# Exclusive decay sums on VectorE, and a state update split between VectorE and GpSimd

## The chip and the metric

The kernel runs on one core of a Trainium2 chip. A core has five engines that matter here: PE (TensorE, matrix multiplication), DVE (VectorE), ACT (ScalarE), POOL (GpSimd) and SP, which only issues transfers. Each works through its own queue of instructions in order, and waits on semaphores for the others. PSUM, where PE writes its results, has 8 banks of 512 float32 per partition; GpSimd has no operand in PSUM anywhere in this kernel.

The metric is the device time of one execution in microseconds (us); less is better. Before the change the median of 7 runs is 213.39 us (212.85 to 214.91).

## What is computed

Two layers, one after the other. The first is a recurrence over 768 steps, for 4 batches and 8 heads of width 40, with a 40 x 40 state per head:

```
for t in range(S):
    y[:, :, t] = einsum('bhd,bhde->bhe', rt, state)
    Sa = einsum('bhde,bhe->bhd', state, at)
    state = state * wt[:, :, None, :] - einsum('bhd,bhe->bhde', Sa, bt) \
            + einsum('bhd,bhe->bhde', vt, kt)
```

The second takes y as x of shape (4, 768, 320) and mixes it over tokens and channels:

```
theta = x @ w_theta
y = einsum('ts,bsd->btd', w_tok_r, x * cos(theta)) + einsum('ts,bsd->btd', w_tok_i, x * sin(theta))
u = x + y
out = u + maximum(u @ w_ch, 0)
```

## The kernel before

The 768 steps of each batch are cut into 6 chunks of 128, so there are N = 24 chunks; chunk i is the chunk `i % 6` of batch `i // 6`. Inside a chunk the recurrence is written as matrix products. Time steps lie on the 128 partitions, and heads and channels (DM = 320 columns) along the free axis. The loops are these:

- `loads(i)` issues the six input loads of a chunk (w, k, b, a, v, and r for two chunks at a time) on SP's queue.
- `prep(i)` makes what a chunk needs before the recurrence. ACT takes the logarithm of w into `lw` (L659). `cs` on PE sums it over time with triangular matrices of ones: L666 with `ntri_inc` gives minus the inclusive sums, L668 with `tri_exc` (the strictly triangular `mask_p`) the exclusive sums, L670 and L674 the total of the chunk, with off-diagonal blocks set to a large negative number. These fill a tile of two PSUM banks, placed so that they are 648 neighbouring columns, and one ACT exp (L678) turns them all into `ex`: the inverse inclusive decay `invW`, the exclusive decay `Wi`, and the decay of the whole chunk `wm`. POOL (DVE for the first two chunks) multiplies k and b by `invW` (kb, L686) and a by `Wi` (ah, L690). PE transposes the results (L616) and ACT copies them out of PSUM (L619).
- `attention_scores(i)` makes 128 x 128 score matrices per head on PE, four kinds in all (`scores`, L740, with 64-row operands, so that PE changes its tiling mode before and after), and DVE multiplies each by a triangular mask (L745). Each uses a two-bank tile.
- `recurrence(i)` makes x0 (from the old state `gt_old` and from v), nx, nu, and, unless the chunk is the last of its batch, the new state: PE adds the old state into the accumulation by a product with the identity (L804, not for the first chunk of a batch), then adds the products of kb with v and nu (L809), and DVE multiplies the sum by `wm` into `gt_new` (egt, L817). The state's transposes (gd) and the next chunk's x0 wait for it.
- `readout(i)` makes the output y on PE (L863 to L872), which DVE multiplies by `Wi` (ex, L879); `theta(i)` makes the angles; `sines` takes cosine and sine on ACT, with another activation table, half a batch at a time, and POOL makes the products z (L924).
- `mix_row` makes one 128-token row of the token mixing of a batch (L942: 12 matmuls of 320 columns) and of the channel mixing (L888), and stores it. The mixer's weights come by POOL's queue (`mixer_weights`, `wtok_block`) and are transposed on PE.

None of this runs in the order of the code. Every operation is added to a `Plan` with an engine, an estimated cost, what it reads and writes, and a priority made of due times (`TIMES`, `OFF`) and a table of single corrections (`ADJ`). `order` builds one static list from these, in which the instructions of every engine then stand. It gives out the PSUM banks too: four banks serve as two double tiles (`ps_d`), the other four as single ones (`ps_s`). In the first microseconds PE gets matmuls on a tile of ones, whose results are not used, ahead of certain operations (`WARM`, L598).

Of the kernel before, what the change touches and what calls it, by code (L numbers as in the profile page):

```python
# [25 lines left out]
WARM = {("tv", 0): (512, 512, 512, 512, 512, 512, 256), ("cs", 0): (256, 128),  # L26
        ("ta", 0): (512, 512, 512, 256, 128), ("spsi", 0): (512, 256, 128), ("cs", 1): (128, 128),
        ("x0", 0): (256, 128)}
# [199 lines left out]
def mm(n):  # L228
    return max(n / 2.4 + 2.5, 25.0)


def tail(n):
# [4 lines left out]
    ah=-35.84, ch=48.62, cs=-41.07, ea=8.9, egd=-133.96, egt=-68.6, ekb=29.91, enu=-49.74,  # L237
    enut=-31.32, er=-1.07, eth=-44.84, eut=-81.74, ev=34.77, ewt=-21.29, ex=-16.18, exp=-69.77,
    ext=-70.75, gd=-0.66, gt=24.57, kb=0.69, la=-21.49, lb=-20.79, lk=-21.05, ln=-58.38,
    loadr=-19.57, lv=-18.31, lw=-23.25, mlu=77.8, mlv=20.57, mphi=99.76, mpsi=106.6, nu=-4.03,  # L240
    nut=17.1, nx=-102.76, oo=44.39, r=13.19, row=39.85, sin=86.4, slu=-21.92, slv=29.13,
    sphi=-34.9, spsi=-25.62, st=34.46, ta=-13.27, th=35.87, tkb=6.76, tr=-5.45, tv=13.16,
    uadd=-11.95, ut=33.59, v=-54.81, wdma=85.37, wt=32.27, x0=-18.91, xt=5.58, y=-25.18,
    z=50.36)
WAIT, TSWITCH, PSWITCH = 398.44, 188399.0, -3357.0
TIMES = dict(
    tile=[
        -65.18, -52.14, -27.19, -15.19, -0.09, 16.27, 18.34, 39.82, 40.75, 43.08, 49.45, 52.18,
        68.94, 83.98, 96.98, 120.81, 109.42, 127.8, 136.07, 145.79, 151.2, 162.31, 163.45,
        185.34],  # L250
    row=[
        43.16, 28.13, 30.47, 7.23, 53.69, 54.58, 93.52, 93.6, 115.41, 121.11, 101.85, 144.65,
        150.48, 155.04, 152.8, 117.63, 86.15, 91.69, 209.97, 231.59, 245.27, 311.99, 320.81,
        183.2],
    rel=[
        -80.1, 35.36, 62.13, 56.14, -154.77, 90.95, 23.01, 50.8])
ADJ = {
    0: 0.01, 1: -0.88, 2: -0.27, 3: -0.13, 4: -9.48, 5: 1.93, 6: 0.01, 7: -6.64, 8: -6.95,
    9: 2.16, 10: -0.5, 11: 4.59, 12: 0.14, 13: 0.14, 14: -2.05, 15: 1.86, 16: 1.1, 17: 0.1,
    18: 0.09, 19: -1.57, 20: -11.2, 21: 2.84, 22: -9.69, 23: 4.35, 24: 11.96, 25: -7.67,  # L260
    26: -8.16, 27: -0.64, 28: 7.64, 29: -2.2, 30: 9.61, 31: -5.25, 32: -7.79, 33: 1.01,
    34: 0.1, 35: 13.97, 36: 2.59, 37: 8.9, 38: -2.75, 39: -7.81, 40: -5.57, 41: -1.21,
    42: -0.06, 43: 0.97, 44: 0.99, 45: 4.55, 46: -1.08, 47: 23.46, 48: 0.44, 49: 12.19,
    50: -0.53, 51: 9.26, 52: -2.79, 53: 0.97, 54: -23.89, 55: 7.88, 56: 2.16, 57: 5.54,
    58: 1.4, 59: 0.22, 60: 1.28, 61: -5.88, 62: -2, 63: -5.35, 64: 13.13, 65: -1, 66: 0.41,
    67: -1.73, 68: 4.62, 69: -0.84, 70: -7.71, 71: -0.16, 72: 4.87, 73: -0.18, 74: 3.79,
    75: 4.43, 76: 0.74, 77: 0.06, 78: 6.38, 79: -6, 80: -2.91, 81: 0.43, 82: 3.27, 83: 3.51,
    84: -0.44, 85: -2.07, 86: -2.74, 87: -2.44, 88: 2.94, 89: -22.98, 90: 3.09, 91: 9.21,
    92: -2.91, 93: 18.56, 94: 11.17, 95: -1.31, 96: -4.33, 97: -0.08, 98: 3.45, 99: 0.12,
    100: -1.86, 101: -0.16, 102: -12.32, 103: 7.19, 104: -6.11, 105: 0.71, 106: -14.73,  # L270
    107: -16.11, 108: -1.26, 109: -2.12, 110: -11.67, 111: 2.03, 112: -15.5, 113: -2.82,
    114: -4.71, 115: -1.47, 116: -2.37, 117: -4.76, 118: 13.45, 119: 10.68, 120: -10.01,
    121: 0.33, 122: 3.27, 123: -1.43, 124: 0.58, 125: -0.44, 126: -0.16, 127: -0.19,
    128: -0.03, 129: 9.47, 130: 3.96, 131: -3.42, 132: 7.74, 133: 20.39, 134: -13.3, 135: -2.8,
    136: -0.48, 137: -9.35, 138: 10.49, 139: -7.17, 140: 0.63, 141: 3.26, 142: -15.88,
    143: -0.69, 144: 2.2, 145: 3.25, 146: -0.52, 147: -2.19, 148: 0.82, 149: -2.89, 150: -2.96,
    151: -1.81, 152: -2.3, 153: 7.23, 154: 2.47, 155: 0.06, 156: 7.19, 157: 4.58, 158: 4.32,
    159: 9.96, 160: -1.9, 161: -3.25, 162: -5.02, 163: -0.81, 164: 6.53, 165: -0.05,
    166: -0.93, 167: -6.53, 168: 5.68, 169: -19.35, 170: -5.08, 171: -3.95, 172: 0.37,
    173: 0.24, 174: -0.2, 175: 0.06, 176: 2.16, 177: 2.88, 178: 0.56, 179: 8.74, 180: 1.39,  # L280
    181: -3.81, 182: 0.11, 183: 0.36, 184: -4.66, 185: 9.47, 186: 2.08, 187: -11.66,
    188: -0.63, 189: 0.85, 190: -0.92, 191: 10.42, 192: -9.45, 193: 13.4, 194: 6.74,
    195: -6.65, 196: -5.88, 197: -0.72, 198: 2.12, 199: -14.95, 200: 3.42, 201: -0.02,
    202: 1.83, 203: -7.04, 204: 6.08, 205: 5.21, 206: -3.71, 207: -2.32, 208: 13.41,
    209: -9.87, 210: 3.64, 211: 10.51, 212: 5.22, 213: 5.88, 214: -4.25, 215: 19.91,
    216: -0.01, 217: 5.8, 218: -8.62, 219: -2.51, 220: 10.26, 221: -2.18, 222: -2.47,
    223: 0.31, 224: -7.04, 225: -7.58, 226: -0.03, 227: -0.65, 228: -0.12, 229: 0.29,
    230: -0.2, 231: -2.85, 232: -6.4, 233: 2.09, 234: 2.03, 235: 0.33, 236: -1.18, 237: 1.09,
    238: 2.44, 239: -1.72, 240: 4.57, 241: 9.13, 242: -7.24, 243: 5.72, 244: -13.82, 245: 4.4,
    246: 0.42, 247: -0.19, 248: -6.12, 249: 1.82, 250: 1.83, 251: 1.17, 252: -1.48,  # L290
    253: -20.54, 254: 7.17, 255: -4.93, 256: 11.2, 257: -1.77, 258: 0.66, 259: -5.47, 260: 1.6,
    261: -0.4, 262: -3.63, 263: -6.81, 264: -3.82, 265: 0.49, 266: 6.09, 267: -2.63, 268: 1.75,
    269: -21.15, 270: 2.29, 271: 5.91, 272: 2.21, 273: 2.4, 274: -0.3, 275: -0.28, 276: -1.01,
    277: -0.05, 278: 0.09, 279: -0.7, 281: 11.01, 282: 0.43, 283: -2.64, 284: -0.86,
    285: -0.06, 286: 1.73, 287: 9.89, 288: 3.49, 289: -0.39, 290: -18.78, 291: 3.31, 292: 4.17,
    293: 4.49, 294: -5.08, 295: 6.91, 296: 3.6, 297: -3.29, 298: 0.56, 299: 10.13, 300: 1.9,
    301: -2.58, 302: -4.97, 303: 1.42, 304: 2.99, 305: -5.36, 306: -7.27, 307: -0.95,
    308: 1.82, 309: -1.14, 310: -0.67, 311: 14.01, 312: -5.86, 313: -0.01, 314: 1.39,
    315: -14.81, 316: -3.16, 317: -9.85, 318: 22.47, 319: -0.79, 320: 0.71, 321: 6.65,
    322: -0.13, 323: -5.53, 324: 7.33, 325: -2.66, 326: 5.7, 327: 1.43, 328: -0.19, 329: -0.19,  # L300
    330: -0.05, 331: -0.22, 332: -0.54, 333: 7.79, 334: -6.85, 335: 33.42, 336: -8.67,
    337: -0.3, 338: -1.27, 339: -5.14, 340: 6.36, 341: 0.65, 342: -20.61, 343: -0.78,
    344: -5.3, 345: -1.21, 346: 9.39, 347: 2.01, 348: -1.89, 349: 10.51, 350: 13.01, 351: -0.2,
    352: -3.48, 353: 4.69, 354: 4.84, 355: -1.57, 356: 1.1, 357: 0.4, 358: -0.66, 359: 0.59,
    360: 7.35, 361: 4.46, 362: -2.04, 363: 4.08, 364: 9.63, 365: 5.54, 366: 7.55, 367: -1.41,
    368: 2.55, 369: 8.31, 370: 0.16, 371: 5.97, 372: -0.62, 373: -2.28, 374: 5.86, 375: -13.84,
    376: -0.34, 377: 1.21, 378: -4.65, 379: 0.4, 380: -1.31, 381: 1.92, 382: -0.18, 383: -0.48,
    384: 0.4, 385: 0.18, 386: -2.48, 387: -14.19, 388: -4.1, 389: 0.04, 390: 0.77, 391: 1.61,
    392: -2.08, 393: -6.37, 394: 0.62, 395: 16.84, 396: 1.46, 397: -1.21, 398: -0.93,
    399: -15.78, 400: -1.89, 401: 7.32, 402: 0.61, 403: -3.23, 404: -4.29, 405: 27.28,  # L310
    406: 1.3, 407: 11.93, 408: -0.22, 409: -2.74, 410: -0.38, 411: 7.07, 412: 0.78, 413: -6.17,
    414: -4.48, 415: -8.05, 416: -4.72, 417: 0.39, 418: -2.8, 419: 10.74, 420: 12.65,
    421: 11.4, 422: 1.61, 423: -5.66, 424: -5.98, 425: 0.9, 426: -1.8, 427: -4.21, 428: -7,
    429: -2.07, 430: 3.36, 431: 4.59, 432: -1.73, 433: -1.81, 434: 6.99, 435: 5.71, 436: 10.27,
    437: 5.14, 438: -0.99, 439: 7.81, 440: 0.8, 441: 1.27, 442: 1.65, 443: 7.35, 444: -5.64,
    445: -1.46, 446: -7.08, 447: 0.09, 448: 13.81, 449: -2.33, 450: 2.41, 451: -7.56,
    452: -0.44, 453: 5.63, 454: 12.16, 455: -15.32, 456: -2.4, 457: 4.6, 458: 1.31,
    459: -12.31, 460: -0.7, 461: -1.77, 462: -0.69, 463: 0.39, 464: 0.12, 465: -1.48,
# [139 lines left out]
def kernel(  # L458
# [144 lines left out]
    def add(eng, kind, i, fn, cost, reads=(), writes=(), at="tile", **kw):  # L603
        if (kind, i) in WARM:
            fn = warmed(kind, i, fn, kw["new"][0])
# [465 lines left out]
```

## Time and profile before

The profiled execution took 213.0 us, with a span of 211.2 us on the core. The busy times:

| Engine | Busy us | Share of the span | Instructions |
|---|---|---|---|
| PE | 198.5 | 94% | 3365 |
| DVE | 166.2 | 79% | 253 |
| ACT | 152.1 | 72% | 342 |
| POOL | 117.6 | 56% | 173 |

The loads and stores on SP's queue moved 27.54 MB and took 66.6% of the time of the 16 DMA engines. Most of their packets are under 512 bytes. These are the lines that the change touches:

| Line | Engine, what | Count | Mean ns |
|---|---|---|---|
| L668 | PE, exclusive sums | 24 | 299 |
| L804 | PE, old state times identity | 16 | 300 |
| L678 | ACT, exp of 648 columns | 24 | 713 |
| L817 | DVE, state times decay | 20 | 486 |
| L598 | PE, matmuls on ones | 21 | 218 to 544 |

A line of the profile's groups gives source line, engine, operation, the tile written and the tiles read with their shapes, the count, the busy time and the mean of one, and then how long the engine sat idle ahead of it and for whom. Matmuls run in a pipeline: their durations overlap, and the starts of neighbours tell more of their price than the durations.

### The profile page before, as it was taken

What the parts mean: (1) busy time and instruction counts of PE and PEld (TensorE: products, weight loads), DVE (VectorE), ACT (ScalarE), POOL (GpSimd) and SP (SyncE); (2) the same over time, 40 slices, a digit from 0 to 9 for tenths busy, and PEclk for the clock granted to TensorE, in tenths of its full rate; (3) what the DMA queues carried; (4) which work ended last, traced back from release to release, by engine and by line L of the source; (5) the groups of instructions that cost most, each with busy time, mean ns of one, the idle gap of its engine ahead of it and who ended that gap; (6) DMA issues with size and microseconds to landing.
All of it is one profiled execution on the core that took longest, in us unless ns stands there. A gap on an engine that the chain in (4) does not pass through costs nothing.

```text
span 211.2 us, 8102 instructions
## 1 busy us (share of the span) xinstructions
PE 198.5 (94%) x3365; PEld 155.6 (74%) x3365; DVE 166.2 (79%) x253; ACT 152.1 (72%) x342; POOL 117.6 (56%) x173
## 2 busy tenths in 40 slices
PE   7668999989999999999999999999999999999993
PEld 3456787767777787788887877788778787877761
DVE  7578778896979799789897677878789898946343
ACT  4475877999799769967948789777898757573011
POOL 3205375798888674895971859763658440751000
PEclk9999999999999999999999999999999999999998
DMA  7999999899999999995979889888997101002122
GB/s 121 196 176 180 153 215 176 143 174 170 198 173 201 192 191 184 175 169 77 260 154 185 168 144 217 141 185 162 215 180 139 34 3 33 3 3 95 70 89 93
DMA packets 134181, 30.82 MB, mean 146 GB/s; under 512 B 125824, under 2 KB 134144, under 8 KB 134144
## 3 DMA queue, kind: packets, MB, share of 16 engines
q1 hardware_dynamic: 131712, 27.54, 66.6%
q0 software_dynamic: 2432, 2.77, 9.1%
q8 instruction: 26, 0.43, 0.8%
q14 instruction: 11, 0.09, 0.1%
HBM read 29.13 MB, written 3.93 MB: 157 GB/s over the span
## 4 chain that ended last, share of the span: by engine, by line
PE 76%; DVE 5%; SPq 5%; ACT 5%; POOL 3%; DMA 2%; issue 2%; ACTq 0%; POOLq 0%; DVEq 0%
PE ps_s L942 19%; PE ps_s L616 13%; PE ps_d L740 10%; PE ps_s L888 9%; SPq L635 4%; PE ps_s L843 4%; DMA raw_w<-in_w_dram 2%; PE ps_s L723 2%; PE ps_s L809 2%; DVE phi L745 2%; PE ps_s L990 2%; PE ps_s L791 2%; PE ps_s L872 2%; ACT ex L678 2%; PE ps_s L870 2%
## 5 line engine op out<-in xcount | busy, mean ns | idle before, releaser
L686 POOL TENSOR_TENSOR kb<-raw_kb,ex 128x320 bf16<-128x320 f32 x44 | 37.2, 862 | 19.1 <-ACT ex L678 17.7
L942 PE MATMUL ps_s<-zr,wtok_r 128*128 128x320 bf16 x144 | 41.0, 300 | 0.0
L942 PE MATMUL ps_s<-zi,wtok_i 128*128 128x320 bf16 x144 | 40.9, 299 | 0.0
L690 POOL TENSOR_TENSOR ah<-raw_a,ex 128x320 bf16<-128x320 f32 x22 | 19.0, 863 | 30.2 <-ACT ex L678 12.7
L745 DVE TENSOR_TENSOR lamu<-ps_d,mask_p 128x1024 bf16<-128x1024 f32 x24 | 29.3, 1219 | 7.0 <-PE ps_d L740 6.6
L745 DVE TENSOR_TENSOR phi<-ps_d,mask_n 128x1024 bf16<-128x1024 f32 x24 | 29.3, 1219 | 4.5 <-PE ps_d L740 4.2
L745 DVE TENSOR_TENSOR lamv<-ps_d,mask_p 128x1024 bf16<-128x1024 f32 x24 | 29.2, 1218 | 3.9 <-PE ps_d L740 3.7
L745 DVE TENSOR_TENSOR psi<-ps_d,mask_p 128x1024 bf16<-128x1024 f32 x24 | 29.2, 1216 | 1.5 <-PE ps_d L740 1.5
L924 POOL TENSOR_TENSOR zi<-cs,x 128x320 bf16<-128x320 f32 x23 | 17.8, 792 | 10.1 <-ACT cs L912 9.9
L924 POOL TENSOR_TENSOR zr<-cs,x 128x320 bf16<-128x320 f32 x23 | 17.8, 792 | 5.8 <-ACT cs L912 5.8
L678 ACT ACTIVATE ex<-ps_d 128x648 f32<-128x648 f32 x24 | 17.1, 713 | 4.8 <-PE ps_d L674 3.6
L619 ACT COPY uT<-ps_s 128x192 f32<-128x192 f32 x24 | 7.5, 319 | 15.5 <-PE ps_s L843 14.2
L879 DVE TENSOR_TENSOR x<-ps_s,ex 128x320 bf16<-128x320 f32 x24 | 11.7, 486 | 7.6 <-PE ps_s L872 3.5
L740 PE MATMUL ps_d<-aT,kbT 64*128 64x128 bf16 x384 | 16.6, 218 | 0.9 <-ACT kbT L619 0.7
L942 PEld LDWEIGHTS <-wtok_r 128*128 128x128 bf16 x144 | 14.0, 97 | 4.5
L942 PEld LDWEIGHTS <-wtok_i 128*128 128x128 bf16 x144 | 14.1, 98 | 3.5
L619 ACT COPY kbT<-ps_s 128x512 f32<-128x512 f32 x24 | 14.2, 590 | 3.3 <-PE ps_s L616 3.2
L952 DVE TENSOR_TENSOR u<-ps_s,x 128x320 bf16<-128x320 f32 x24 | 11.7, 489 | 6.0 <-PE ps_s L942 5.3
L961 DVE SCALAR_TENSOR_TENSOR oo<-ps_s,u 128x320 f32<-128x320 f32 x24 | 11.6, 488 | 5.2 <-PE ps_s L888 4.5
L870 PE MATMUL ps_s<-kb,lamv 128*128 128x40 bf16 x192 | 15.4, 181 | 0.0
L872 PE MATMUL ps_s<-kb,lamu 128*128 128x40 bf16 x192 | 15.0, 180 | 0.1
L616 PE MATMUL ps_s<-ident,kb 128*128 128x128 bf16 x192 | 14.7, 220 | 0.1
(117 smaller groups left out, 562.1 us busy)
## 6 DMA issues: line engine op xcount, KB each, us to landing
raw_v<-in_v_dram SPq DMA_DIRECT2D x24, 160.0 KB, 3.7
raw_w<-in_w_dram SPq DMA_DIRECT2D x24, 160.0 KB, 4.6
raw_kb<-in_k_dram SPq DMA_DIRECT2D x24, 160.0 KB, 3.8
raw_a<-in_a_dram SPq DMA_DIRECT2D x24, 160.0 KB, 4.6
raw_kb<-in_b_dram SPq DMA_DIRECT2D x24, 160.0 KB, 4.4
raw_r<-in_r_dram SPq DMA_DIRECT2D x24, 160.0 KB, 3.4
out_dram<-oo SPq DMA_DIRECT2D x24, 160.0 KB, 2.3
wrow_i<-in_moe_w_tok_i_dram POOLq DMA_DIRECT2D x6, 192.0 KB, 4.9
```

Of the source, the lines that this page charges most:

```text
L616: nc.tensor.transpose(out=dst[:, c:c + 128], in_=pair(src, g), identity=ident)
L619: nc.scalar.copy(out=out.bitcast(FP32), in_=in_)
L678: add("ACT", "exp", i, lambda: nc.scalar.activation(out=ex, in_=ps(pk).rearrange("p a b -> p (a b)")[:, 512 - DM:512 + DM + 8], func=AF.Ex ...
L686: lambda j=j: (nc.vector if fast else nc.gpsimd).tensor_tensor(out=paired(kb[:, j])[:, :, :, 0:D], in0=natural(raw_kb[s4][:, j]), in1=invW ...
L690: lambda: (nc.vector if fast else nc.gpsimd).tensor_tensor(out=paired(ah)[:, :, :, 0:D], in0=natural(raw_a[i % 6]), in1=Wi, op=ALU.mult),
L740: nc.tensor.matmul(t[:, q, g, :], lhsT=lhs[rows(q), g * 128:(g + 1) * 128], rhs=rhs[rows(q), g * 128:(g + 1) * 128], start=True, stop=True)
L745: add("DVE", kindm, i, lambda: nc.vector.tensor_tensor(out=dst.rearrange("p a b c -> p (a b) c"), in0=ps(p).rearrange("p a (g c) -> p (a g ...
L870: nc.tensor.matmul(o, lhsT=lamv[:, p, g, :], rhs=kb[:, 0, h, 0:D], start=first, stop=False, skip_group_check=True)
L872: nc.tensor.matmul(o, lhsT=lamu[:, p, g, :], rhs=kb[:, 1, h, 0:D], start=False, stop=True, skip_group_check=True)
L888: nc.tensor.matmul(dst, lhsT=lhs[:, kt, :], rhs=rhs[:, kt, :], start=kt == 0, stop=kt == 2)
L924: nc.vector if fast else nc.gpsimd).tensor_tensor(
L942: nc.tensor.matmul(ps(pk)[:, 0:DM], lhsT=wtok[nm][:, s, j * 128:(j + 1) * 128], rhs=zs[c][:, s], start=n == 0 and c == 0, stop=n == NT - 1 ...
```

## The change

It has four parts.

1. The exclusive sums are no longer made by PE. L668 goes. The inclusive sums and the totals (328 columns) now fit one bank, and `cs` takes a single bank instead of a double tile. Since the exclusive sum is the inclusive one less the step's own logarithm, DVE adds `lw` to minus the inclusive sum (`wi`, into the new tile `sx`), and a second exp on ACT with scale -1 makes `Wi` into the new tile `we` (`ew`). The exp of the inclusive sums and the total keeps its place, and `wi` is ordered after it. ah (L690) and the output multiplication (L879) read `we` in place of `ex`.
2. From chunk 4 on, for chunks that are neither first nor last of a batch (13 of them), PE does not add the old state by the identity (L804). DVE adds it when it takes the sum out of PSUM, into a new float32 tile `sum`, and POOL multiplies by `wm` into the new state (`wgt`). The other chunks keep the old way.
3. The matmuls on ones at the start are placed by the plan's own times, in steps of 128 columns wherever the plan leaves PE idle before 14 us, instead of a written list.
4. All due times, priorities and corrections of the plan are replaced (`OFF`, `TIMES`, `ADJ`, and the three weights), so that the order of instructions changes on every engine.

```diff
-WARM = {("tv", 0): (512, 512, 512, 512, 512, 512, 256), ("cs", 0): (256, 128),
...
+FROM_POOL = 4
+WARM_FROM, WARM_TO, WARM_STEP = 1450.0, 14000.0, 107.0
...
-            nc.tensor.matmul(t[:, 0, 512 - DM:512], lhsT=ntri_inc, rhs=lw[:, :, 0:D],
+            nc.tensor.matmul(t[:, 0:DM], lhsT=ntri_inc, rhs=lw[:, :, 0:D],
                              start=True, stop=True)
-            nc.tensor.matmul(t[:, 1, 0:DM], lhsT=tri_exc, rhs=lw[:, :, 0:D],
-                             start=True, stop=True)
...
-        add("ACT", "exp", i, lambda: nc.scalar.activation(
-            out=ex, in_=ps(pk).rearrange("p a b -> p (a b)")[:, 512 - DM:512 + DM + 8],
-            func=AF.Exp), 710, [pk], [kex], table="lnexp")
+        got = add("ACT", "exp", i, lambda: nc.scalar.activation(
+            out=ex, in_=ps(pk)[:, 0:DM + 8], func=AF.Exp), 440, [pk], [kex], table="lnexp")
+        kw, we, sx = ("we", i % NEX), we_t[i % NEX], sx_t[i % 2]
+        add("DVE", "wi", i, lambda: nc.vector.tensor_tensor(
+            out=sx.rearrange("p (h d) -> p h d", h=H),
+            in0=ps(pk)[:, 0:DM].rearrange("p (h d) -> p h d", h=H), in1=lw[:, :, 0:D], op=ALU.add),
+            490, [pk, ("lw", s2)], [("sx", i % 2)], after=[got])
+        add("ACT", "ew", i, lambda: nc.scalar.activation(out=we, in_=sx, func=AF.Exp, scale=-1.0),
+            455, [("sx", i % 2)], [kw], table="lnexp")
...
+            by_pool = not first and i >= FROM_POOL
+            join = not first and not by_pool
...
-                if not first:
+                if join:
                     nc.tensor.matmul(t[:, 0:DM], lhsT=ident,
...
+            if by_pool:
+                add("DVE", "egt", i, lambda: nc.vector.tensor_tensor(
+                    out=sum_t, in0=grown(),
+                    in1=gt_old.rearrange("p g c d -> p (g c) d")[:, :, 0:D], op=ALU.add), 490,
+                    [gk, ("gt", (i + 1) % 2)], [("sum", 0)])
+                add("POOL", "wgt", i, lambda: nc.gpsimd.tensor_tensor(
+                    out=new_state, in0=sum_t, in1=wm.to_broadcast([128, 8, D]), op=ALU.mult), 830,
+                    [("sum", 0), ("ex", i % NEX)], [("gt", s2)])
...
+    idle = WARM_FROM
     for o in order:
+        if o.eng == "PE" and o.start < WARM_TO:
+            if o.new is not None:
+                t = ps(o.new[0])
+                t = t[:, 0] if len(t.shape) == 3 else t
+                for _ in range(int((o.start - idle) / WARM_STEP)):
+                    nc.tensor.matmul(t[:, 0:128], lhsT=busy[:, 0:128], rhs=busy[:, 0:128],
+                                     start=True, stop=True, skip_group_check=True)
+            idle = o.start + 1.5 * o.cost + 50
```

## The prediction

> **What bounds the kernel now.** I read the page's busy times and slices first, then the same engines in five stretches cut at the landmarks of the trace, then who waited for whom in each stretch.
>
> ```profile
> PE 198.5 (94%) x3365; PEld 155.6 (74%) x3365; DVE 166.2 (79%) x253; ACT 152.1 (72%) x342; POOL 117.6 (56%) x173
> ...
> PE   7668999989999999999999999999999999999993
> ...
> DVE  7578778896979799789897677878789898946343
> ACT  4475877999799769967948789777898757573011
> ...
> DMA  7999999899999999995979889888997101002122
> ```
>
> PE is at 94%, but the average hides two regimes, which the stretches show (columns: length, then busy time and instructions of PE, weight loads, DVE, ACT, POOL, then granted clock, DMA share, GB/s):
>
> ```profile
> 0.00:24.00 24.00, 18.17 (x265) 12.55 (x265) 17.12 (x61) 14.45 (x32) 7.00 (x19) 1.00 0.95 171
> 24.00:56.00 32.00, 29.86 (x597) 24.21 (x594) 26.81 (x31) 27.54 (x66) 24.28 (x33) 1.00 0.95 173
> 56.00:71.00 15.00, 13.74 (x285) 11.60 (x283) 13.92 (x18) 13.40 (x30) 11.20 (x18) 1.00 1.08 192
> 71.00:163.00 92.00, 91.93 (x1620) 74.22 (x1617) 76.16 (x98) 74.56 (x167) 62.49 (x88) 1.00 0.93 175
> 163.00:206.00 43.00, 43.00 (x601) 32.12 (x599) 30.39 (x47) 21.54 (x51) 12.60 (x16) 1.00 0.12 41
> ```
>
> From 71.0, when the first token-mixing row (L942) issues, to 206, PE is busy 134.93 of 135 us, and the waits of PE list none in that time. There a PE instruction removed is time removed, as long as the others still feed it. Before 71 PE has gaps (its listed waits sum to 7.8 us, behind ACT, DVE and the start), DVE is at 84 to 93% and the DMA engines at 95% and more: several things share the limit there. The last input load is issued at 159.0, so that 43 us of PE work follow the loads: the end is PE's.
>
> A matmul's row overstates its price, since matmuls overlap. The decay sums of one chunk in the timeline (start, duration):
>
> ```profile
> 144.52 0.30 PE L666 MATMUL ps_d<-lw,ntri_inc 128*128 128x320 bf16 x1
> 144.66 0.30 PE L668 MATMUL ps_d<-lw,mask_p 128*128 128x320 bf16 x1
> 144.79 0.17 PE L670 MATMUL ps_d<-off_diag,ident 128*128 128x8 bf16 x1
> ```
>
> The next one starts 0.133 us after L668, not 0.30. So L668 costs 0.133 us of PE, and by the same width so does L804.
>
> **What goes from PE.** 24 matmuls of L668, and 13 of the 16 of L804 (chunks 4 and up that are neither first nor last of a batch): 37 x 0.133 = 4.9 us (by their means of 300 ns it would be 11.1, which the timeline refutes). I split them at the first row, since only behind it is PE the limit.
>
> Behind it stand 13 of L668 and 10 of L804: 23 x 0.133 = 3.06 us less. But the instructions are reordered as a whole. In the built order of the changed kernel a little more of the other work stands behind the first row: eight more L779 matmuls, eight L791, four L773 and four transposes, six more transposes of the mixer's weights, eight scores fewer: at their issue intervals (columns / 2.4 GHz at the granted clock of 1.00, at least 0.025; 0.034 a score) +0.8 us. And PE goes between the 64-row scores (L740) and full-height matmuls 77 times there, instead of 70. One such switch costs about 0.1 us (the last L872 starts at 146.08, the first score at 146.19, where 0.03 would do): +0.7. Sum behind the first row: -3.06 + 0.8 + 0.7 = **-1.6 us**.
>
> Ahead of it 11 of L668 and 3 of L804 go: 14 x 0.133 = 1.9 us. Worth between all of it (PE is busy for 92% of 56 to 71) and nothing (DMA and DVE set the pace). I take half, **-0.9**. The warm-up matmuls (21 before, 3.0 us at issue intervals; 68 of 128 columns, 3.6 us after) lie in PE's idle start, cover: the first chunk's loads and vector work. I cost them at 0; if that cover fails, +0.6.
>
> **What comes on DVE.** 24 additions from PSUM to SBUF at 128x320. The nearest row is L817, same shape and sources, 486 ns. Back to back it is less:
>
> ```profile
> 26.00 1.23 DVE L745 TENSOR_TENSOR lamu<-ps_d,mask_p 128x1024 bf16<-128x1024 f32 x1
> 27.14 1.22 DVE L745 TENSOR_TENSOR lamv<-ps_d,mask_p 128x1024 bf16<-128x1024 f32 x1
> 28.27 0.48 DVE L879 TENSOR_TENSOR x<-ps_s,ex 128x320 bf16<-128x320 f32 x1
> ```
>
> Masks follow each other by 1.13, and where the timeline has a 320-wide one followed at once it is 0.40. So +9.6 us of DVE in all, 0.4 a chunk. Behind the first row 12 to 14 of them, 5.4 us, fall on a DVE with 28.5 us idle: covered, 0. Ahead of it: up to the output multiplication of chunk 5 (sixth L879, 55.5), from which the first batch's sines and so the first row follow, the new order has 10 additions and one more mask but one state update fewer, 4.7 us; DVE is idle for 5.2 of the 32 us from 24 to 56 and for more before. Between 0 and +4.7. I take 0, because the idle time is just enough and the row start has slack of its own (theta of chunk 5 is evacuated at 58.9, and its sines start at 63.1, behind other ACT work and a table load).
>
> **ACT.** One exp of 648 columns (713 ns) becomes one of 328 and one of 320. Nearest rows: 128x320 ACTIVATE and COPY, 427 to 478. Sum 0.9, i.e. +0.18 by durations and +0.1 after the overlap of 0.1 that each ACT instruction has with the next; x24 = 2 to 4.5 us on an engine with 17 us idle behind the first row: 0. The table loads stay at 14. ah now waits for exp, addition and second exp: about 1 us more than before. Behind it in POOL's queue stand kb and v of later chunks, and PE's transposes of ah. But the new order has 3 to 10 us of PE work between a chunk's decay sums and its ah transposes (before: 1.2 to 5.6), so that stays covered.
>
> **The state update.** L817 stays one DVE instruction (now an addition, same sources and shape). Behind it comes a GpSimd multiplication, 13 times, and what waits is x0 and the state's transposes on PE, and whatever stands behind it in POOL's queue (kb, ah, z). The rows:
>
> ```profile
> L690 POOL TENSOR_TENSOR ah<-raw_a,ex 128x320 bf16<-128x320 f32 x22 | 19.0, 863 | 30.2 <-ACT ex L678 12.7
> L924 POOL TENSOR_TENSOR zr<-cs,x 128x320 bf16<-128x320 f32 x23 | 17.8, 792 | 5.8 <-ACT cs L912 5.8
> L817 DVE TENSOR_TENSOR gt<-ps_s,ex 128x320 bf16<-128x320 f32 x20 | 9.7, 486 | 2.9 <-PE ps_s L809 2.4 <-ACT nuT L619 0.4
> ```
>
> A rule speaks against this move: the Trainium skill, "GPSIMD Engine Reference", section Engine selection, gives two-input elementwise work to VectorE because GpSimd is about twice as slow. That would be 0.97 us each; the rows here say 0.79 to 0.86, I take 0.83. From the end of L809's issue to the new state: 0.17 for the last matmul, 0.49, 0.83, and about 0.05 for each of three handovers (kbT's copy ends at 8.72, the scores that wait for it start at 8.78): 1.65 us by the rows, 1.8 by the rule, 0.76 before. In the new order PE has between 1.8 and 3.3 us of other work there. By the rows the shortest cover just holds; by the rule it is used up, with nothing left for a DVE caught in a 1.2 us mask. I cost it at 0. POOL's +10.8 us fall on an engine at 56%.
>
> **PSUM and queues.** The decay sums leave the two-bank tiles, which then serve only scores, and take one of the four single banks for some 1.5 us per chunk. No row prices this; between -0.3 us (scores find a bank sooner) and +1 (a transpose waits), I take 0. On SP's queue raw_w of chunk 0 stands third instead of second: ln starts a load later, about 1 us, but kb needs the fifth load in either order (L686 at 7.12), and only ah moves behind both kb on DVE: +0.4, if nothing absorbs it in the stalls of the first 24 us. I leave it at 0. Of POOL's DMAs only the place of wch and of the weight rows (L982) among kb and z shifts; they are needed from 71 on and issue from 56 on. 0.
>
> **Sum.** -1.6 - 0.9 = -2.5 us on the profiled execution's own 213.0 (span 211.2 and 1.8 around it): 210.5. That execution was 0.4 below the median of the runs, so I say **210.8**.
>
> **Rivals.**
> 1. *Early work counts in full*, and the switches are fewer than I price: -3.06 + 0.8 - 1.9 = -4.2, 208.8 to 209.2. For it: PE is busy for 93% from 24 to 71. Against: those busy times contain overlap, and the added vector work falls in the same place. 0.18.
> 2. *DVE becomes the bound before the first row* (the slower end). The 4.7 us do not fit, chunk 5's output and the first row come late by them, and PE starts its unbroken run from there: -1.6 + 4.7 = +3.1, 216.5. It decides from a delay of 1.6 us on, where the gain behind the row is spent. For it: DVE was busy 13.92 of 15 us from 56 to 71. Against: 5 us idle before, and the slack at the sines. 0.15.
> 3. *The state chain through POOL stalls PE*: 10 times after 71, at 0.5 us (half a mask or kb ahead in a queue) +5, less 2.5: 215.9. For it: covers of 1.8 to 2.3 against a chain of 1.65. Against: before, covers of 0.7 to 1.2 against 0.76 gave no wait. 0.06.
> 4. *Nothing measurable*: the vector work eats the early gain and about 1 us more, 212.4 to 214.4. 0.14.
>
> **Numbers.** The likeliest, 210.8 (its own range 209.2 to 212.3), gets 0.47. The range 207.5 to 214.8 leaves out the far ends of rivals 1 to 3. About 0.5% (1.1 us) is what a measurement can tell from no change. Faster: 0.47 nearly whole and 0.18: 0.65. Same 0.14, slower 0.21.
>
> **What would show it.** After: PE again without listed waits from the first row to the end, with the first row at 70 to 71; two PE lines gone; DVE near 178 us of busy time, POOL near 128. Wrong would be: a first row at 73 or later with DVE full ahead of it (rival 2), or PE waits on GpSimd's new state line (rival 3), or waits for a PSUM bank.

## The result, and the profile after

The changed kernel takes **212.25 us** (median of 13 runs, 211.4 to 213.63) against 213.68 us for the kernel before (34 runs). The ratio is 0.9934, with a 95% interval of 0.9915 to 0.9954: 0.7% faster, and 1.4 us where 2.9 had been forecast. The profiled execution took 211.47 us with a span of 209.7.

The page of the changed kernel, its busy times and slices (as shown of before):

```profile
PE 194.9 (93%) x3375; PEld 156.6 (75%) x3375; DVE 173.7 (83%) x277; ACT 154.4 (74%) x366; POOL 127.4 (61%) x186
...
PE   7778998798999999999999999999999999999993
...
DVE  7499968799999797998788778989999997657533
```

PE's share fell by one point and DVE's and POOL's rose, as meant. In slices PE still looks full from the first row on; a digit of 9 only says 90% or more, and what is missing is smaller than that. The stretches at the same landmarks (columns: length, then busy time and instructions of PE, weight loads, DVE, ACT, POOL, granted clock, DMA share, GB/s):

```profile
0.00:24.00 24.00, 19.26 (x323) 16.31 (x323) 19.69 (x66) 15.31 (x37) 7.89 (x20) 1.00 0.93 168
24.00:56.00 32.00, 27.48 (x582) 22.53 (x576) 27.68 (x34) 27.99 (x71) 25.09 (x35) 1.00 1.01 182
56.00:71.00 15.00, 14.31 (x287) 11.56 (x285) 14.49 (x20) 13.91 (x32) 13.25 (x20) 1.00 1.06 189
71.00:163.00 92.00, 90.97 (x1652) 74.24 (x1650) 81.53 (x112) 74.56 (x179) 64.40 (x92) 1.00 0.92 171
163.00:206.00 43.00, 42.53 (x551) 31.95 (x549) 29.38 (x47) 22.62 (x52) 16.76 (x23) 1.00 0.13 44
```

From 71 to 163 PE stands at 90.97 of 92 us, where it stood at 91.93; from 163 to 206 at 42.53 of 43. There are 1.5 us in which PE idles, in the very part where it was to stay full and before had 0.07. PE's waits from 71 on, of which before listed none (columns: who waits for whom, total us, times, longest):

```profile
PE ps_d L750 <- DVE psi L755: 0.3, 1, 0.3
PE ps_s L910 <- ACT uT L625: 0.3, 1, 0.3
PE ps_s L865 <- DVE u L974: 0.2, 1, 0.2
PE ps_s L783 <- ACT xT L625: 0.2, 1, 0.2
```

Four single waits on four different tiles, and none of them is a tile that the change adds. The groups of the change's own instructions and of the row L924 of before (now L946):

```profile
L700 POOL TENSOR_TENSOR ah<-raw_a,we 128x320 bf16<-128x320 f32 x22 | 19.0, 863 | 5.9 <-ACT we L689 3.0 <-issue 1.0 <-POOL gt L837 0.6
L946 POOL TENSOR_TENSOR zr<-cs,x 128x320 bf16<-128x320 f32 x23 | 17.8, 791 | 14.1 <-ACT cs L934 14.1
L685 DVE TENSOR_TENSOR sx<-ps_s,lw 128x320 f32<-128x320 f32 x24 | 11.5, 484 | 4.7 <-ACT ex L682 4.7
L837 POOL TENSOR_TENSOR gt<-sum,ex 128x320 bf16<-128x320 f32 x13 | 9.4, 723 | 7.6 <-DVE sum L833 7.1 <-DMA raw_kb<-in_b_dram 0.5
```

The new addition takes 484 ns, as its neighbour did before. The state's decay on POOL takes 723 ns, less than the 0.83 us of the nearest rows, and POOL stands idle for 7.1 us in all ahead of it, waiting for DVE: it is not POOL that is late there.

The time splits well at two landmarks: the start of the first token-mixing matmul (L942 before, L964 after), here called the first row, and the start of the last one, called the last row.

| Profiled execution | First row | Last row | Between them |
|---|---|---|---|
| before | 70.96 | 205.57 | 134.61 |
| before, a second execution (d1) | 72.35 | 206.90 | 134.55 |
| after | 69.16 | 204.06 | 134.90 |
| after, a second execution (a1) | 69.91 | 204.71 | 134.80 |

In both kernels 5.6 us of the span follow the second landmark. Two executions of one kernel differ by up to 1.4 us, and all of that lies ahead of the first row; the length behind it repeats to 0.1 us. So the gain lies **ahead of the first row**, and behind it, where the forecast had -1.6 us, the changed kernel is 0.2 to 0.3 longer.

### The profile page after: what moved, and what is told of

It is laid out like the page before. It is cut to its first block, busy times and chain, and to the rows that moved or that the text cites. A ratio compares the mean times of both kernels' runs of the same rounds, so it can differ in the third digit from the quotient of the medians.

```text
span 209.7 us, 8135 instructions
## 1 busy us (share of the span) xinstructions
PE 194.9 (93%) x3375; PEld 156.6 (75%) x3375; DVE 173.7 (83%) x277; ACT 154.4 (74%) x366; POOL 127.4 (61%) x186
## 4 chain that ended last, share of the span: by engine, by line
PE 60%; DVE 14%; ACT 12%; POOL 5%; issue 5%; DMA 3%; POOLq 0%; DVEq 0%; ACTq 0%
PE ps_s L964 15%; PE ps_s L622 10%; PE ps_d L750 8%; PE ps_s L910 7%; PE ps_s L865 3%; DMA wrow_i<-in_moe_w_tok_i_dram 3%; DVE psi L755 3%; ACT L934 2%; PE ps_s L1064 2%; DVE phi L755 2%; ACT cs L934 2%; PE ps_s L801 2%; PE ps_s L894 2%; DVE lamu L755 2%; DVE lamv L755 2%
## 5 line engine op out<-in xcount | busy, mean ns | idle before, releaser
L696 POOL TENSOR_TENSOR kb<-raw_kb,ex 128x320 bf16<-128x320 f32 x44 | 37.7, 870 | 21.6 <-ACT aT L625 9.5
L964 PE MATMUL ps_s<-zr,wtok_r 128*128 128x320 bf16 x144 | 40.7, 300 | 0.0
L964 PE MATMUL ps_s<-zi,wtok_i 128*128 128x320 bf16 x144 | 40.7, 299 | 0.0
L946 POOL TENSOR_TENSOR zr<-cs,x 128x320 bf16<-128x320 f32 x23 | 17.8, 791 | 14.1 <-ACT cs L934 14.1
L700 POOL TENSOR_TENSOR ah<-raw_a,we 128x320 bf16<-128x320 f32 x22 | 19.0, 863 | 5.9 <-ACT we L689 3.0
L974 DVE TENSOR_TENSOR u<-ps_s,x 128x320 bf16<-128x320 f32 x24 | 11.6, 488 | 10.7 <-PE ps_s L964 10.7
L946 POOL TENSOR_TENSOR zi<-cs,x 128x320 bf16<-128x320 f32 x23 | 17.9, 791 | 1.3 <-ACT cs L934 1.3
L750 PE MATMUL ps_d<-aT,kbT 64*128 64x128 bf16 x384 | 17.2, 218 | 0.9 <-ACT aT L625 0.4
L964 PEld LDWEIGHTS <-wtok_r 128*128 128x128 bf16 x144 | 14.0, 98 | 4.2
L964 PEld LDWEIGHTS <-wtok_i 128*128 128x128 bf16 x144 | 14.1, 98 | 3.8
L685 DVE TENSOR_TENSOR sx<-ps_s,lw 128x320 f32<-128x320 f32 x24 | 11.5, 484 | 4.7 <-ACT ex L682 4.7
L750 PEld LDWEIGHTS <-kbT 64*128 64x128 bf16 x384 | 11.2, 94 | 4.8 <-issue 1.5
```

Of the source, the lines that this page charges most:

```text
L696: lambda j=j: (nc.vector if fast else nc.gpsimd).tensor_tensor(out=paired(kb[:, j])[:, :, :, 0:D], in0=natural(raw_kb[s4][:, j]), in1=invW ...
L700: lambda: (nc.vector if fast else nc.gpsimd).tensor_tensor(out=paired(ah)[:, :, :, 0:D], in0=natural(raw_a[i % 6]), in1=Wi, op=ALU.mult),
L750: nc.tensor.matmul(t[:, q, g, :], lhsT=lhs[rows(q), g * 128:(g + 1) * 128], rhs=rhs[rows(q), g * 128:(g + 1) * 128], start=True, stop=True)
L946: nc.vector if fast else nc.gpsimd).tensor_tensor(
L964: nc.tensor.matmul(ps(pk)[:, 0:DM], lhsT=wtok[nm][:, s, j * 128:(j + 1) * 128], rhs=zs[c][:, s], start=n == 0 and c == 0, stop=n == NT - 1 ...
L974: add("DVE", "uadd", q, lambda: nc.vector.tensor_tensor(out=u[:, 0:DM], in0=ps(pk)[:, 0:DM], in1=x[:, 0:DM], op=ALU.add), 488, [pk, ("x", ...
```

## Experiments: the PE work and the new vector work

The theories at the start: that DVE, now busier behind the row, is late with its results; that POOL's state decay is; or that PE's work was mispriced. Four kernels tell them apart: the change again (a1), the PE work back (a2), and each of the two new pieces of vector work cut short (a3, a4).

**a1**, the changed kernel itself, for the comparison on one chip.

> The changed kernel itself, as the reference on this chip for the three kernels beside it. Expected: 212.2 us in the median, 0.7% under the kernel before, as in its first runs.

Measured: 212.24 us, ratio to before 0.9954 (0.9929 to 0.9979).

**a2** gives PE back 37 matmuls of 320 columns, at the places of the old ones; the accumulation that follows overwrites what they write.

```diff
             nc.tensor.matmul(t[:, 0:DM], lhsT=ntri_inc, rhs=lw[:, :, 0:D],
                              start=True, stop=True)
+            nc.tensor.matmul(t[:, 0:DM], lhsT=ident, rhs=busy[:, 0:DM], start=True, stop=True,
+                             skip_group_check=True)
...
+                if by_pool:
+                    nc.tensor.matmul(t[:, 0:DM], lhsT=ident, rhs=busy[:, 0:DM], start=True,
+                                     stop=True, skip_group_check=True)
```

> The changed kernel in its own order of instructions, with the PE work that the change removed put back without use: a 320-column matmul on the tile of ones ahead of the decay sums of each chunk (24) and ahead of the state products of the 13 chunks whose state goes through GpSimd, in a bank that the next matmul overwrites. Nothing new waits for another engine. If PE's issue still bounds the stretch behind the first row (theory A and B alike), the 23 of them behind it cost 23 x 0.133 = 3.1 us and the 14 ahead of it between 0 and 1.9: +3.1 to +4.9 us over the changed kernel. If another engine has become the bound there (the rival of the slower end), PE has idle time for them: under +1.5 us.

Measured: 214.89 us, 1.0088 (1.0056 to 1.0119), which is 2.65 us over a1 and less than the 3.1 to 4.9 expected. The first row came at 69.77, against 69.91 in a1 and 69.16 in after, and the length behind it was 137.31, against 134.80. So the 23 matmuls behind the row cost 2.5 us, 0.11 each, where 0.133 was priced; the missing 0.5 us may have filled gaps, since PE's listed waits behind the row fell from 1.0 us to 0.3. The 14 ahead of it cost **little**: of the 2.65 us between the medians 0.15 is left for them, and the row's place, which moves by 0.75 us between two executions of the changed kernel, can't tell it more finely. The mechanism that the forecast rests on is there, behind the first row only.

**a3** lets the new addition work on 40 of its 320 columns. The exclusive decays of seven heads are left uncomputed.

```diff
-            out=sx.rearrange("p (h d) -> p h d", h=H),
-            in0=ps(pk)[:, 0:DM].rearrange("p (h d) -> p h d", h=H), in1=lw[:, :, 0:D], op=ALU.add),
+            out=sx[:, 0:D], in0=ps(pk)[:, 0:D], in1=lw[:, 0, 0:D], op=ALU.add),
```

> Same order of instructions, but the new addition on DVE takes 40 of its 320 columns, so that the exclusive decays of the other seven heads are not computed (their tile is filled once, by GpSimd, with a constant). The 24 instructions fall from 0.49 to some 0.12 us, their place, waits and banks stay. Theory A (the fuller DVE hands its results late, and PE's new gaps of 1 to 2 us behind the first row come from that): -1 to -2 us against the changed kernel, most of it behind the first row. Theory B (the gaps come from the new order itself, its switches and waits, and DVE has room): within 0.4 us. Theory C (the state chain through GpSimd): within 0.4 us.

**a4** lets POOL's state decay work on 5 of each block's 40 columns. The rest of the new state is left out.

```diff
-                    out=new_state, in0=sum_t, in1=wm.to_broadcast([128, 8, D]), op=ALU.mult), 830,
+                    out=new_state[:, :, 0:5], in0=sum_t[:, :, 0:5],
+                    in1=wm.to_broadcast([128, 8, 5]), op=ALU.mult), 830,
```

> Same order of instructions, but the new GpSimd multiplication takes 5 of 40 columns of each block, so that the rest of the state of those 13 chunks is left as an earlier chunk wrote it. It falls from some 0.83 to some 0.2 us. Theory C (the longer chain to the next state makes PE wait): -1 us or more against the changed kernel. Theories A and B: within 0.4 us, since PE has 1.8 to 3.3 us of other work in between.

Measured: a3 212.06 us, 0.9932 (0.9902 to 0.9963), length behind the row 134.53; a4 211.82 us, 0.9943 (0.9922 to 0.9964), length 135.02. Both lie within 0.5 us of a1, and the intervals overlap. Neither the time of the addition on DVE nor that of the decay on POOL is what the missing gain went into.

## Where the 1.7 us behind the row went

With a2 to a4 the price of PE's work was roughly confirmed and the two obvious costs were excluded. So the lengths were taken apart. For every pair of neighbours on PE behind the first row I took start to start, less what the first of them usually occupies, less 0.11 us where the 64-row mode is entered or left. Before: 122.5 us of work, 70 switches (7.7), 4.4 us of gaps. After: 120.3 us of work, 77 switches (8.5), 6.1 us of gaps. The work fell by 2.2 and the switches rose by 0.8, both as forecast. **The gaps rose by 1.7**, which the sum has no term for. How much of a length is called work or gap depends on what is taken as usual; the rise does not. With another such price, the median start to start of each shape, work falls by 2.1 us and the gaps rise by the same 1.7, and the gaps over 0.15 us sum to 0.7 us (4 of them) before and to 2.9 us (11) after.

They stand at fixed places. In after, a1, a3 and a4 the larger of them are the same to 0.02 us: 0.44 ahead of a channel-mixing product (L910), 0.33 ahead of u's transposes, 0.30 ahead of an x0, 0.28 ahead of a decay sum and of another x0, 0.47 ahead of scores. f1 and c1 (below), whose first rows come 2 to 3 us later, have these gaps again to 0.03. Only the wait of a weight row's transposes (L1012) changes from one execution to the next, between nothing in a3 and 0.4 us in a4. The first of them, in the timeline of a1 (start, duration):

```profile
102.26 1.28 ACT L934 ACT_TABLE_LOAD   x1
...
103.56 1.10 ACT L934 ACTIVATE cs<-th,pi_col 128x960 f32<-128x960 f32 x1
...
104.16 0.50 PE L1012 MATMUL ps_s<-ident,wrow_i 128*128 128x128 bf16 x6
104.56 0.30 ACT L625 COPY uT<-ps_s 128x192 f32<-128x192 f32 x1
...
104.92 0.58 PE L910 MATMUL ps_s<-wch,uT 128*128 128x320 bf16 x3 [0.26 <-ACT uT L625]
```

Behind the six transposes of L1012 stands L910, which needs uT. ACT copies uT only when its instruction of 103.56 (L934, one of the angle functions) is nearly through, and that one started as the table load ended. None of these instructions is of the change; they stand so because the order was made anew.

**c2** moved six of the stalled PE operations back in the order, so that other work would stand in the gaps (c3 did the same and cut the warm-up, below).

```diff
+LATER = (("ch", 4, 2), ("ut", 5, 1), ("x0", 14, 1), ("cs", 19, 1), ("x0", 20, 1), ("slu", 20, 1))
...
+        pe = [m for m in range(n + 1, len(order)) if order[m].eng == "PE"]
+        m = pe[behind - 1]
...
+        order.insert(m, order.pop(n))
```

> The changed kernel with six operations of PE moved one or two places back in its queue, each one ahead of which PE stood for 0.3 to 0.47 us in four runs of this order alike (mixing products of one row behind the copy of uT, one transposition of u, x0 of chunks 14 and 20, the decay sums of the twentieth place, the scores with nu of the twenty-first). Nothing else moves. If the gaps behind the first row are such single misplaced waits, the stretch from the first to the last row falls by 0.8 to 1.7 us and the time to 210.5 to 211.4. If they only turn up at the next instruction, because a late engine sets the pace, within 0.4 us of the changed kernel.

Measured: 213.45 us, 0.9994 (0.9972 to 1.0015), length behind the row 136.2: the gaps grew. PE's longest waits from 70 on in c2:

```profile
PE ps_s L623 <- POOL kb L697: 0.7, 1, 0.7
PE ps_s L623 <- DVE u L975: 0.6, 1, 0.6
PE ps_s L623 <- ACT aT L626: 0.4, 1, 0.4
```

The stalls moved on to transposes (L623), one waiting for POOL's kb, the others for DVE and ACT. An operation that is moved makes others late. That the gaps come with the order, and not with one engine, is what a3, a4 and c2 support; that a better order of the same operations would be rid of them was not shown.

## Order or parts: four runs that could not tell

b1 gives the new order's tables (`OFF`, `TIMES`, `ADJ`, weights) and its warm-up to the old operations, b2 the old tables to the new operations, b4 keeps the new decay sums but the old state on PE, under the new tables. Since `ADJ` goes by an operation's number, the numbers were kept aligned.

```diff
+        o.old = None if kind in ("wi", "ew", "wgt") else self.old
...
-            o.prio = 1000.0 * (TIMES[o.spec[0]][o.spec[1]] + OFF[o.spec[2]] + ADJ.get(o.idx, 0.0))
+            o.prio = 1000.0 * (TIMES[o.spec[0]][o.spec[1]] + OFF[o.spec[2]] + ADJ.get(o.old, 0.0))
...
-            by_pool = not first and i >= FROM_POOL
+            by_pool = False
```

(The first two hunks are of b2, the last is of b4.)

> The old way of computing (exclusive sums and old state by PE, one exp of 648 columns) planned with the new due times, corrections and warm-up rule; the corrections keep their operations. If the new tables themselves carry the cost behind the first row (theory T: more switches and more small gaps because of the tables), the first row comes near 70 us and the stretch from the first to the last row takes some 137 us, as in the run with the PE work put back: 214.5 to 215.5 us. If the gaps come with the new parts (theory P), this order has none of them and the old work: about 213, first to last row 135 us.

> The new way of computing planned with the old due times and corrections and the old written warm-up list; the three new operations get their kind's offset and no single correction. Theory T: first to last row takes 134.6 - 2.5 = 132 us, the first row stays at 71: 210.5 to 211.5 us, faster than the changed kernel. Theory P (the gaps belong to the new parts under any order): first to last row 134 to 135 us, and the first row at 71 or later because of the fuller DVE: 213 us or more.

> The changed kernel with the decay sums by DVE, but with the state as before (old state added by PE through the identity, decay by DVE, nothing on GpSimd), planned with the new tables. PE gets 13 matmuls of 320 columns back, 10 of them behind the first row: by the price of the put-back run (2.5 us for 23) +1.1 us there, against -0.3 for a shorter chain. Expected 212.8 to 213.6 us. If the state part is worth nothing, 212.2.

Measured: b1 228.32 us (1.0692), b2 219.93 (1.0292), b4 225.42 (1.0540). All three miss every expectation. The first row of b1 came at 77.24; behind it b1 took 143.1 us, b2 140.5 and b4 149.0, against 134.6 to 135. In these three cases the table of single corrections did not fit another set of operations than the one it was made for. These runs show that mixing costs 6 to 15 us, and cannot say how the 1.7 us divide between order and parts. That stays open.

## Ahead of the first row: warm-up and loads

**b3** takes all matmuls on ones away (`WARM_TO` at 0).

```diff
-WARM_FROM, WARM_TO, WARM_STEP = 1450.0, 14000.0, 107.0
+WARM_FROM, WARM_TO, WARM_STEP = 1450.0, 0.0, 107.0
```

> The changed kernel without any of the 68 matmuls on ones at the start; all else in the same order. The prediction put the warm-up at nothing, with 0.6 us at most for the additional ones: expected within 0.5 us of the changed kernel. If they hold the granted clock, the first profile slices show a lower clock and the time is longer by a few tenths to 3 us.

Measured: 214.72 us, 1.0051 (1.0024 to 1.0078), 2.5 us over a1 by the medians (2.1 by the ratios), where the prediction had the warm-up at 0 with 0.6 if its cover failed. In the profiled execution the first row came at 71.40, 1.5 us after that of a1 and 2.2 after that of after, and the length behind it was 135.92, 1.1 more than in a1. That second part is nearly all one wait: 0.9 us ahead of L1012 for the transfer of a weight row. Whether it belongs to the missing warm-up was not tested. In b3's timeline of PE (start, duration):

```profile
5.93 0.42 PE L672 MATMUL ps_s<-lw,ntri_inc 128*128 128x320 bf16 x1 [5.93 <-ACT lw L665]
...
12.59 1.02 PE L733 MATMUL ps_s<-ident,r 128*128 128x128 bf16 x8
...
16.06 0.47 PE L672 MATMUL ps_s<-lw,ntri_inc 128*128 128x320 bf16 x1
16.32 0.21 PE L674 MATMUL ps_s<-off_diag,ident 128*128 128x8 bf16 x1
```

The 320-column matmul takes 0.47 us and holds PE for 0.26, twice the 0.133 of later; eight transposes take 1.02 instead of 0.61. PE runs at half rate until about 17.7 us, though the granted clock of these stretches is given as 1.00. This figure misleads: the trace's first clock record, at the full clock, begins at 17.84, and a stretch without a record is printed as 1.00. In after and a1 the first record begins at 5.61 and 6.89. The Trainium skill, "TensorE: Matmul & The Clock Gate", Part 1, has the rule behind this: the array starts at half clock and gets the full one only after some 3.4 us of sustained activity, counted in a window that runs freely. The trace agrees: PE was busy for 93% of the last 3.41 us ahead of 17.84, and for 74 to 75% of each of the two such stretches before it, which did not bring the full clock. The page's remark that such a ramp is below 1% of a typical kernel is not contradicted: the 1.5 to 2.2 us at the first row are 0.7 to 1.0% of 212 us.

**f1** undoes part 3 of the change alone: the 21 matmuls of the old list in the new order (those ahead of v's transposes, which came first in the old order, now ahead of the first decay sum). **f2** makes part 3 alone, in the kernel before.

```diff
-WARM_FROM, WARM_TO, WARM_STEP = 1450.0, 14000.0, 107.0
+WARM_LIST = {("cs", 0): (512, 512, 512, 512, 512, 512, 256, 256, 128),
+        ("ta", 0): (512, 512, 512, 256, 128), ("spsi", 0): (512, 256, 128), ("cs", 1): (128, 128),
+        ("x0", 0): (256, 128)}
```

> The changed kernel with the 21 wider matmuls on ones of the old list (the seven that stood ahead of v's transposes now ahead of the first decay sum, which comes first in the new order) in place of the 68 of 128 columns. Theory W, the new rule for them brings the first row forward: first row at 71 or later, ratio to before about 1.000. Theory O, the new order does it and the rule is worth nothing by itself: first row at 69 to 70, ratio 0.993 to 0.996 as the change's own. Behind the first row 134.5 to 135 us by either.

> The kernel before, in its old order and with its old parts, with the new rule for the matmuls on ones (64 of 128 columns by the plan's own times instead of 21 wider ones). Theory W: first row at 69.5 to 70.5 instead of 71.0 to 72.4, ratio 0.994 to 0.996. Theory O: first row at 71 to 72.4, ratio 0.998 to 1.002. Behind the first row 134.6 us by either.

Measured: f1 214.15 us, 1.0048 (1.0028 to 1.0069), first row at 72.47, length 134.80. f2 212.97 us, 1.0003 (0.9977 to 1.0030), first row at 70.64, length 134.86. Neither theory as it stood: the rule is worth 2.0 to 2.4 us in the new order (1.0048 less a1's 0.9954 or the first result's 0.9934, of 213 us), all of the gain and more, and nothing in the old one. PE's timeline in f1 tells why:

```profile
1.46 3.27 PE L1065 MATMUL ps_s<-busy 128*128 128x512 bf16 x9 [1.46 <-DVE off_diag L540]
6.14 0.43 PE L674 MATMUL ps_s<-lw,ntri_inc 128*128 128x320 bf16 x1 [1.41 <-ACT lw L667]
...
7.56 0.61 PE L624 MATMUL ps_s<-ident,v 128*128 128x128 bf16 x4 [0.88 <-ACT v L707]
8.54 1.03 PE L624 MATMUL ps_s<-ident,kb 128*128 128x128 bf16 x8 [0.37 <-DVE kb L698]
...
12.28 1.04 PE L752 MATMUL ps_d<-aT,kbT 64*128 64x128 bf16 x16
```

and the same operations in a1:

```profile
6.23 0.47 PE L672 MATMUL ps_s<-lw,ntri_inc 128*128 128x320 bf16 x1
...
7.70 0.40 PE L622 MATMUL ps_s<-ident,v 128*128 128x128 bf16 x4 [0.38 <-ACT v L705]
...
8.68 0.62 PE L622 MATMUL ps_s<-ident,kb 128*128 128x128 bf16 x8 [0.31 <-DVE kb L696]
```

In the new order the first decay sum comes about 1.2 us later than in the old (6.14 and 6.23 against 4.95), because w's logarithm does. The old list ends at 4.73, PE idles for 1.41 us, and stays at half rate until about 14 (the first clock record begins at 13.95). In a1 the rule fills the time up to the sum, and v's transposes at 7.70 run at full rate. In the old order the old list had no such hole (the first clock record of before begins at 5.02, that of f2 at 4.29), which fits f2's having nothing to gain.

**c1** gives the new order the old one's first loads on SP's queue; **d2** gives the kernel before the new one's (w of chunk 2 three places earlier).

```diff
+    slots = [n for n, o in enumerate(order) if o.eng == "SP"][:17]
+    first = sorted((order[n] for n in slots), key=lambda o: LOADS.index((o.kind, o.i)))
+    for n, o in zip(slots, first):
+        order[n] = o
```

> The changed kernel in its own order, but the first 17 loads on SP's queue stand in the order of the kernel before (w of chunk 0 second instead of third, of chunk 1 eighth instead of seventh, of chunk 2 thirteenth instead of eleventh). If the earlier start of the first row (69.2 to 69.9 us instead of 71.0) comes from the new order of the first loads, it goes: decay sums of chunk 2 at 16 to 17 us instead of 15, first row at 71, and the time rises by 0.5 to 1.5 us. If it comes from the rest of the new order or from the shorter PE work there, within 0.4 us.

> The kernel before with one change: among its first loads, w of chunk 2 is issued three places earlier (after k of chunk 1) and k, b and v of chunk 1 trade places accordingly. Nothing else moves. If the order of the first loads is what brings the first row forward in the changed kernel, whatever the new parts are, the decay sums of chunk 2 come at 16 to 16.6 instead of 17.06, the first row 0.5 to 1 us earlier, and the time falls by 0.3 to 1 us. If the first row hangs on the rest of the old order, within 0.3 us.

Measured: c1 213.97 us, 1.0019 (0.9995 to 1.0043), first row at 72.14, length 134.62. d2 213.31 us, 1.0004 (0.9981 to 1.0027), first row at 71.39, length 134.67: its third decay sum came at 16.33 instead of 17.06, and nothing of that shows at the row. In c1 w of chunk 2 is issued at 11.53 instead of 8.07, PE waits 1.3 us for its logarithm, and then this (stretches, columns as above):

```profile
12.00:14.00 2.00, 1.26 (x25) 0.88 (x23) 1.94 (x4) 1.97 (x5) 0.00 (x0) 1.00 0.84 131
14.00:16.00 2.00, 0.74 (x14) 0.52 (x11) 1.40 (x3) 0.87 (x4) 0.00 (x0) 0.80 1.07 181
16.00:20.00 4.00, 3.96 (x57) 3.29 (x56) 2.82 (x5) 2.24 (x6) 1.84 (x3) 0.50 1.12 232
20.00:24.00 4.00, 3.52 (x54) 2.51 (x52) 3.26 (x4) 2.31 (x6) 1.76 (x3) 0.74 1.09 192
```

PE was busy for only 0.74 of the 2 us before 16, and the granted clock fell to 0.50 from 15.22 to 22.05. In this execution the late load's wait of 1.3 us was thus followed by 6.8 us at the half clock, and the row came 2.2 us later than in a1. How these 2.2 us divide between the two was not measured.

**c3** is c2 with at most 41 matmuls on ones ahead of any operation, so that the first decay sum is not held up by them; **d1** is a second execution of the kernel before (no edit).

```diff
-                for _ in range(int((o.start - idle) / WARM_STEP)):
+                for _ in range(min(int((o.start - idle) / WARM_STEP), WARM_MOST)):
```

> As the kernel beside it, and at most 41 instead of 45 matmuls on ones ahead of the first decay sums, which in the run whose matmuls ran slowly for longest kept the sums back from 5.93 to 6.23 us. Expected: the decay sums at 5.9 in every run, and 0 to 0.3 us less than the kernel beside it; if PE's rate rises later for the smaller number, 0.3 to 1 us more.

> The kernel before, profiled once more: how far its first row (70.96) and its stretch to the last row (134.61 us) repeat. Expected within 0.5 and 0.3 us.

Measured: c3 213.92 us, 1.0025 (1.0002 to 1.0047); the first sum came at 5.85, and no time was gained over c2. d1: 214.35 us in its single execution; its landmarks are in the first table.

No run that computes the whole result was faster than the changed kernel.

## Why the prediction failed

The direction was right and the time fell inside the range, but of the 2.9 us forecast (213.68 to 210.8) 1.4 came. The prediction's own sum is -2.5; the rest is that the median of before rose from 213.39 to 213.68 with more runs, and rounding. Point by point:

- **Behind the first row, -1.6.** Its three terms hold: work less by 2.2 (-3.06 + 0.8), switches +0.8 (priced 0.7), and a2 gives 0.11 us for a matmul there where 0.133 was priced. What failed is the sum's silence: the prediction costed the additions, the exps, the state chain and the PSUM banks at 0 each by naming a cover for each, and took PE as gapless because the waits listed none. But before had 4.4 us of gaps there, each below what a list of waits shows, and the changed kernel has 6.1. A fully new static order was priced by counting what moves, and not by where each operation stands to its producer. This is the step that failed, by 1.7 us, and with it the sign "PE again without listed waits". How the 1.7 us divide between the new order and the new parts stays open.
- **Ahead of the row, -0.9.** The first row did come earlier: 69.2 to 70.3 in five executions with the new parts and order (after, a1 to a4), 70.6 to 72.4 in four of the old order (before, d1, d2, f2), 1.5 us by the means. But the reason given, 14 matmuls less, is worth little (about 0.15 us by a2): that a gain of the forecast's size and more came here is luck. In the new order the early row depends on the new warm-up (f1) and on the new first loads (c1). Which places in the new order make it earlier than the old order with the same warm-up (f2) was not found.
- **Warm-up at 0.** Wrong as a price. Its cover was named as other engines' work, but what it buys is PE's rate in the microseconds that follow (f1: half until about 14). Whether the new list still reached up to the first decay sum, and at what rate the matmuls behind it ran, was the question to ask.
- **Loads on SP at 0, +0.4 at worst.** w of chunk 2, which moved forward, was not looked at; with the old loads c1 loses the gain, in the profiled execution with a second stretch at the half clock.
- **DVE, ACT and POOL at 0.** Right as far as a3 and a4 test it: the new work's own length costs nothing. ACT was not tried alone.
- **The state chain through POOL.** No PE wait on it; the multiplication is 0.72 us, shorter than the 0.83 taken and than the 0.97 of the rule.
- **The rivals.** The early work in full is spoken against by a2. DVE as the bound ahead of the row would have given a row at 73 or later: it came at 69 to 70. POOL's chain as a stall is refuted by the waits. The 212.25 us lie between the upper end of the likeliest case (212.3) and the lower end of "nothing measurable" (212.4), and neither mechanism was right: both have most of the gain behind the row, and there it is not.
- **The other signs.** POOL 127.4 us (forecast 128) and both PE lines gone. DVE 173.7 us, not 178: neighbours on DVE overlap in the record, so 24 times 0.484 added 7.5 us, not 11.6. The prediction itself had 9.6 in one place and 11.6 in this sign.

Read in sum, over the executions above: 1.5 us earlier at the row, 0.1 longer behind it (means 134.81 and 134.67, a2 left out), so -1.4, the measured gain. With starts that vary by up to 1.4 us from one execution to the next, that it fits to the tenth is luck.

## What to carry to other kernels

Where a change makes a hand-tuned or planned order anew, count the gaps of the limiting engine start by start before and after, the ones below the list of waits too: here the saved work was bought back in tenths of a microsecond at a dozen places. The warm-up of this kernel belonged to the order it was written for, so after any change of the order check in the durations of the first 20 us whether PE runs at full rate. And under a table of single corrections mixing halves told nothing here; add or cut one cost in place, as a2 to a4 do.

## What was not expected of the hardware

- The granted clock as printed does not show a PE that is cold from the start: in b3 and f1 it reads 1.00 while 320-column matmuls hold PE for 0.26 to 0.27 us instead of 0.133, because the first clock record begins at 17.84 and 13.95 only. Where a record exists, in c1, it reads 0.50 for the same half rate.
- The start of one and the same kernel varies: the 45 matmuls on ones of the changed kernel took 4.65 us in one execution and 4.98 in another, with the first decay sum at 5.94 at full rate (0.30 us) or at 6.23 at half rate (0.47). The first row then came at 69.16 and at 69.91. The first clock record begins at 5.61 in the one and at 6.89 in the other.
- A wait of 1.3 us was enough for the half clock: in c1 PE was busy for 56% of the 3.41 us ahead of 15.22, and 6.83 us at 0.50 followed.
